# A planner that counts transfers in flight, and reciprocals of the third pair of heads spread by matrix products

## The chip, the cores and the metric

The kernel runs on one core of a Trainium2 chip. A core has five engines, each with its own row of instructions that it works off in order: TensorE (matrix products, PE in the profile, its weight loads PEld), VectorE (DVE), ScalarE (ACT), GpSimd (POOL) and SyncE (SP, which here only starts transfers). They wait for one another by semaphores. Data move between DRAM and the on-chip memory by DMA transfers that an engine issues; the queues are those of SyncE and GpSimd. TensorE writes to eight banks of its own (128 partitions x 512 floats each), from which VectorE and ScalarE read.

The metric is the device time of one execution in microseconds. Before the change three runs took 1011.58, 1011.61 and 1008.52 us, median 1011.58.

## The reference

Causal attention with a decay, for 8 batches x 8 heads, 576 positions, 64 numbers per head, then a two-layer network over all 4608 rows. All numbers are float32.

```python
scores = (1 / sqrt(64)) * q @ k.T                      # per batch and head
cum    = cumsum(log(clip(f, 1e-4, 1)))                 # f: one number per position
scores = where(later position, -1e9, scores + cum[:, None] - cum[None, :])
scores = scores - max(scores)
attn   = exp(scores);  attn = attn / (sum(attn) + 1e-9)
x      = (attn @ v)                                    # heads side by side: 4608 x 512
h      = x @ w_in                                      # 512 x 2048   (FFN1)
g      = max(h, 0) + alpha * min(h, 0)
out    = g @ w_out                                     # 2048 x 512   (FFN2)
```

## The kernel before

**Pairs of heads.** Attention is done for two heads at a time; 32 pairs, n = 0 to 31, four to a batch. For a pair TensorE makes the scores (q by k, five blocks of query rows, the last of 64 rows called the tail), VectorE adds the decay and takes the row's extreme (lines 609, 703 and 846), ScalarE takes the exponential and its row sums (571, 826). The first nine pairs (`attention`) turn the exponentials round by TensorE transposes (584, 651, 725), the other 23 (`turned`) by VectorE transposes (883) and 16 DMA moves (920), half of them issued by SyncE and half by GpSimd. Then come the value products with v, and ScalarE copies the result to `xs` (758, 959).

**Reciprocals.** The row sums of a pair lie down the partitions, and the values have the positions along the row. So the reciprocals (649) are transposed to nine rows of 128 (651), copied to `bR` (652) and spread over the partitions into `ri`, of which there is one buffer. For most pairs that is a store to DRAM (657) and three broadcast loads (1000, function `fetch`). The fourth pair (n = 3, `hurry`) does it by six products with a selecting matrix `sel` into two banks (function `quick`), and two VectorE copies (642) from there to `ri`. GpSimd multiplies `xs` by `ri` (979), ScalarE and GpSimd split the result into a high and a low part `xx` (988, 989): this is x of the pair, the input of FFN1.

**FFN1 and FFN2.** For a batch of 512 rows FFN1 has 16 chunks, each with two halves of six products of 512 columns: the first half takes x of the batch's first two pairs, the second half that of the last two. Nine such batches (the ninth gathers all 64-row tails) make 1728 products; their results go to DRAM (1039) and come back for FFN2, which runs when attention is over and has nothing but TensorE, VectorE and ScalarE work beside loads. While attention runs, FFN1's products fill TensorE between the products of the pairs.

**The order.** No order is written by hand. The kernel describes some 4170 operations, each with an engine, a cost in nanoseconds, a key, the operations it waits for and the buffers it takes; class `Plan` then plays the engines through: of all ready operations it takes the one that can start earliest, and of equal ones that with the lowest key. Every cost is first multiplied by a number drawn between 0.97 and 1.03 from one random sequence, operation by operation (`SEED`), so that one operation more or less shifts the draws of all that follow. A transfer ends when one common channel, at 220 or 280 bytes per nanosecond, has taken it. Rings of buffers (`Ring`) hold an operation back until one is free; the banks of transposes and spreading products are ring `rT`, of at most three. The order in which the planner takes the operations is the order of each engine's instructions; the waits in the program follow from the data alone. Up to 75 us, where the planner foresees TensorE idle for over 0.5 us, it also writes fillers (466), products of the identity matrix into a bank about to be used.

All products are written through the helper at line 364, so that their rows in the profile are told apart by tile names: `rqk` and `Qhl` are scores, `big,vr` values, `xx,wi` FFN1, `big,sel` spreading products.

Of the kernel before, what the change touches and what calls it, by code (L numbers as in the profile page):

```python
# [19 lines left out]
NP = H // 2  # L20
# [69 lines left out]

SLACK = {"DVE": 1.12, "ACT": 1.08, "POOL": 1.05}
ENGS = ("PE", "ACT", "DVE", "POOL", "SP", "-")


class Plan:
    def __init__(self):
        self.now = dict.fromkeys(ENGS, 0.0)
        self.chan = 0.0
        self.ops = []
        self.banks = self.fill = None  # L100
        self.rnd = random.Random(SEED)
# [27 lines left out]
    def run(self):  # L129
        ops, self.ops = self.ops, []  # L130
        cand = {e: [] for e in ENGS}
        for o in ops:
            if o.n == 0:
                cand[o.eng].append(o)
        left = len(ops)
        mine = set(ops)
        while left:
            best = None
            for e in ENGS:
                t0 = self.now[e]  # L140
                pick = None
                for o in cand[e]:
                    r = o.ready
                    for b in o.bufs:
                        if b.t is not None:
                            continue
                        k = b.seq - b.ring.next
                        if k and not any(o2.ring is b.ring and o2.seq == b.ring.next for o2 in o.bufs):
                            r = None
                            break  # L150
                        a = b.ring.at(k)
                        if a is None:
                            r = None
                            break
                        if a > r:
                            r = a
                    if r is None:
                        continue
                    s = t0 if t0 > r else r
                    if pick is None or (s, o.key) < pick[:2]:  # L160
                        pick = (s, o.key, o)
                if pick is not None and (best is None or pick[0] < best[0]):
                    best = pick
            assert best is not None, "the plan is stuck"
            s, _, o = best
            self.t = s
            cand[o.eng].remove(o)
            left -= 1
            end = s + o.ns
            t0_, new = self.now[o.eng], []  # L170
            if o.two:
                end += max(0.0, self.now["POOL"] - s)
            self.now[o.eng] = end
            if o.kb:
                self.chan = max(self.chan, s + 1.4) + o.kb / (220.0 if s < FAR else 280.0)
                end = self.chan + (0.0 if s < 4 else 2.0)
            o.start, o.end = s, end
            for b in o.bufs:
                if b.t is not None:
                    continue  # L180
                st = b.ring.store
                f = min(st.free)
                st.free.remove(f)
                b.i, b.t = f[1], st.items[f[1]]
                if o.eng == "PE" and st is self.banks:
                    new.append((f[0], b.t))
                b.ring.next += 1
                b.ring.held += 1
            if new and self.fill and s < FILL:
                self.fill(new[0][1], s - max(t0_, new[0][0]))  # L190
            o.fn()
            for b in o.bufs:
                b.left -= 1
                b.last = max(b.last, end)
                if b.left == 0:
                    b.ring.held -= 1
                    b.ring.store.free.append((b.last + 0.3, b.i))
            for c in o.outs:
                c.n -= 1
                c.ready = max(c.ready, end + self.lag(o, c))  # L200
                if c.n == 0 and c in mine:
                    cand[c.eng].append(c)
# [3 lines left out]
def attention_moe(  # L206
# [120 lines left out]
    def c_dve(n):  # L327
        return 75 + n / 0.96
# [216 lines left out]
    def attention(n):  # L545
# [2 lines left out]
        k0 = NS * n  # L548
        kl, kc = k0 - 16, k0 - 7
        hurry = HURRY if n == NP - 1 else 0  # L550


        held = []
# [70 lines left out]
        bri = Buf(rri)  # L624
        ri_ops = []

        def quick(bR, r_, key):

            bB = [Buf(rT), Buf(rT)]
            at = lambda c0: bB[c0 // 512].t[:, c0 % 512 : c0 % 512 + (128 if c0 < 512 else 64)]  # L630

            def prods():
                R9 = bR.t[0:9]
                for i in range(4):
                    mm(at(128 * i), sel[:, i], R9, True, True)
                mm(at(512), sel[:, 4], R9[:, 0:64], True, False)
                mm(at(512), sel[:, 5], R9[:, 64:128], False, True)

            q_ = op("PE", 1400, prods, key, [r_, o_sel], bB + [bR])
            quick_ops.append(q_)  # L640
            for c0, c1 in ((0, 512), (512, S)):
                ri_ops.append(op("DVE", c_dve(c1 - c0), lambda c0=c0, c1=c1: ve.tensor_copy(flat(bri)[:, c0:c1], bB[c0 // 512].t[:, 0 : c1 - c0]), key, [q_], [bB[c0 // 512], bri]))

        def quotients(key):

            bT, bR = Buf(rT), Buf(rR)
            both = lambda: su()
            q_ = op("ACT", 230, lambda: ac.activation(both(), both(), AF.Identity, bias=eps), key, sums + [o_eps], [bst])
            q_ = op("DVE", 190, lambda: ve.reciprocal(both(), both()), key, [q_], [bst])
            q_ = op("-", 400, lambda: None, key, [q_])  # L650
            t = op("PE", 109, lambda: pe.transpose(bT.t[0:9, 0:128], both(), ident), key, [q_, o_id], [bT, bst])
            r_ = op("ACT", c_act(128), lambda: ac.activation(bR.t, bT.t[0:9, 0:128], AF.Copy), key, [t], [bT, bR])
            if hurry:
                quick(bR, r_, key)
                return
            d = rd[n % 3][0 : 128 * 9]
            st_ = op("SP", 350, lambda: sy.dma_start(d.rearrange("(c q) -> c q", q=128), bR.t), key, [r_], [bR], kb=4.5)
            ri_ops.extend(fetch(key, st_, d, bri))
# [102 lines left out]
        v_deps = lambda: e1 + e2[0] + e2[1] + e3 + [e4, o_zero] + l_v  # L761

        def rest():
            st = k0 + 11.5 - hurry
            late = ri_ops if n < NN else [op("-", 2000, lambda: None, st, ri_ops)]
            quotient(n, bxs, bri, xs_ops[0] + xs_ops[1] + late, st)

# [24 lines left out]
            done(value_ops[-1])  # L792
        else:
            behind.append(values)
        quotients(k0 + 11 - hurry)
        later_x.append(rest)
        if n < NE - 1:
            for f_ in later_x:
# [7 lines left out]
    def turned(n):  # L806
# [110 lines left out]
        for i in range(16):  # L917
            a, k = i // 4, i % 4
            q_, n_ = (po, "POOL") if i % 2 else (sy, "SP")
            moves.append(op(n_, 550 if i % 2 else 450, lambda a=a, k=k, q_=q_: q_.dma_start(  # L920
                bM.t[32 * k : 32 * k + 32, a], t_t[32 * a : 32 * a + 32, k, 32 * TA * bTa.i : 32 * TA * bTa.i + CW]),
                k0 + 8.05, turns, [bTa, bTb, bM], kb=100))

# [476 lines left out]
```

## Time and profile before

| | before |
|---|---|
| three runs | 1011.58, 1011.61, 1008.52 us |
| profiled execution | 1010.48 us, its span 1008.7 us |
| TensorE busy | 999.0 us (99%) |
| weight loads busy | 888.5 us (88%) |
| VectorE, ScalarE, GpSimd busy | 803.7, 606.8, 394.6 us |
| TensorE in the chain that ended last | 93% |

The profiled execution is one of its own; the span runs from the first to the last instruction that the profile shows, and 1.8 us lie around it. A row in order of time gives the start, the time from its start to the end of the last of its instructions, the line, the tiles and the count; in square brackets stands the idle time before it and what ended it. Matmuls are pipelined and their ends modelled, so rows of TensorE overlap by a little. A float32 product that the program has once stands as two matmuls in the trace.

### The profile page before, as it was taken

Reading aid. Unit: us, or ns where it says so; the run is one execution under the profiler, and the core shown is the slowest. Engines: PE = TensorE matmul, PEld = TensorE weight load, DVE = VectorE, ACT = ScalarE, POOL = GpSimd, SP = SyncE. Lnnn points to the kernel's source line nnn. Section 1 sums busy time; section 2 is a strip of 40 time slices with the busy share of each in tenths; the row PEclk is TensorE's granted clock in tenths of the full one; section 3 lists DMA queues with packets and bytes.
Section 4 is the critical chain, followed back from the end, with each engine's and each line's share of the span. In section 5 each row is a group of like instructions: output and inputs, shape, how many; then the busy total and the mean of one; then the engine's idle time right before and its main releaser. Section 6 shows DMA issues by size and latency. Waiting matters only on the chain.

```text
span 1008.7 us, 22200 instructions
## 1 busy us (share of the span) xinstructions
PE 999.0 (99%) x7900; PEld 888.5 (88%) x7900; DVE 803.7 (80%) x1745; ACT 606.8 (60%) x1369; POOL 394.6 (39%) x635
## 2 busy tenths in 40 slices
PE   9999999999999999999999999999999999999998
PEld 6778888888888788888888888999999999999998
DVE  7878768888877848868655987788898888989994
ACT  7987876666666645656444766564554645546551
POOL 4575758799988858869740100000000000000000
PEclk9999999999999999999999999999999999999999
DMA  7988748889887887968766666633534344434411
GB/s 225 264 241 245 227 130 230 238 250 264 257 242 211 260 242 206 260 206 233 235 174 241 212 205 212 207 116 123 157 113 142 115 140 132 139 115 137 135 55 42
DMA packets 130686, 191.12 MB, mean 189 GB/s; under 512 B 22088, under 2 KB 79728, under 8 KB 130576
## 3 DMA queue, kind: packets, MB, share of 16 engines
q1 hardware_dynamic: 124400, 170.66, 55.7%
q0 software_dynamic: 5888, 18.85, 7.4%
q8 instruction: 62, 1.02, 0.4%
q14 instruction: 48, 0.39, 0.1%
q10 hardware_dynamic: 288, 0.20, 0.1%
HBM read 102.74 MB, written 48.80 MB: 150 GB/s over the span
## 4 chain that ended last, share of the span: by engine, by line
PE 93%; DMA 3%; DVE 2%; ACT 1%; SPq 1%; POOL 1%; issue 0%; DVEq 0%; ACTq 0%
PE bank L364 89%; PE bank L584 2%; DMA big<-big 1%; SPq L920 1%; DVE big L883 1%; DMA rd<-st 0%; DMA vr<-in_vv_dram 0%; PE bank L432 0%; DMA rqk<-in_qk_dram 0%; ACT big L826 0%; DVE Z L491 0%; PE bank L466 0%; POOL Z L510 0%; ACT big L580 0%; POOL Qhl L538 0%
## 5 line engine op out<-in xcount | busy, mean ns | idle before, releaser
L364 PE MATMUL bank<-xx,wi 128*128 128x512 f32 x1728 | 407.7, 392 | 1.8 <-DVE st L846 1.8
L364 PEld LDWEIGHTS bank<-xx,wi 128*128 128x128 f32 x1728 | 319.8, 188 | 68.4 <-DVE st L846 2.2
L826 ACT ACTIVATE big<-big,st 128x384 f32<-128x384 f32 (+4 forms) x207 | 118.6, 575 | 44.3 <-DVE st L846 44.3
L1037 DVE SCALAR_TENSOR_TENSOR hs<-bank,sa,hs 128x512 f32<-128x512 f32 x96 | 71.2, 743 | 79.0 <-ACT hs L1035 78.8
L364 PE MATMUL bank<-wi,gh 128*128 128x256 f32 x1008 | 123.9, 283 | 0.0
L364 PE MATMUL bank<-wot,gh 128*128 128x256 f32 x1008 | 123.9, 283 | 0.0
L364 PEld LDWEIGHTS bank<-wot,gh 128*128 128x128 f32 x1008 | 122.3, 192 | 0.1
L364 PEld LDWEIGHTS bank<-wi,gh 128*128 128x128 f32 x1008 | 122.3, 192 | 0.0
L1035 ACT ACTIVATE hs<-bank,ab 128x512 f32<-128x512 f32 x96 | 66.1, 689 | 88.3 <-PE bank L364 70.5
L883 DVE STREAM_TRANSPOSE big<-big 128x1408 f32<-128x1408 f32 (+2 forms) x69 | 86.6, 1273 | 22.3 <-DMA hd<-hs 6.7
L364 PEld LDWEIGHTS bank<-big,vr 128*64 128x64 f32 x1884 | 88.9, 137 | 12.0 <-issue 3.9
L364 PE MATMUL bank<-big,vr 128*64 128x128 f32 (+2 forms) x1884 | 95.5, 259 | 2.0 <-DVE st L609 1.1
L538 POOL TENSOR_TENSOR Qhl<-rqk,Qhl 128x640 fp32r<-128x640 f32 (+1 forms) x56 | 83.3, 1496 | 30.8 <-ACT Qhl L537 29.1
L920 POOL DMA_DIRECT2D big<-big x184 | 92.1, 507 | 7.9 <-DVE big L883 4.2
L364 PE MATMUL bank<-Qhl 64*128 64x512 f32 (+6 forms) x840 | 93.1, 326 | 0.1
L364 PEld LDWEIGHTS bank<-Qhl 64*128 64x128 f32 (+1 forms) x840 | 74.9, 186 | 15.8 <-issue 9.1
L510 POOL TENSOR_TENSOR Z<-Z,tri 128x384 f32<-128x384 f32 x60 | 54.6, 922 | 27.9 <-DMA Z<-c 18.5
L364 PE MATMUL bank<-wot,xx 128*128 128x256 f32 x504 | 62.4, 283 | 0.0
L364 PE MATMUL bank<-wi,xx 128*128 128x256 f32 x504 | 62.4, 283 | 0.0
L364 PEld LDWEIGHTS bank<-wi,xx 128*128 128x128 f32 x504 | 61.3, 192 | 0.0
L364 PEld LDWEIGHTS bank<-wot,xx 128*128 128x128 f32 x504 | 61.3, 192 | 0.0
L1032 ACT ACTIVATE hs<-bank,sg 128x512 f32<-128x512 f32 x48 | 33.0, 687 | 33.3 <-PE bank L364 28.4
(176 smaller groups left out, 1501.5 us busy)
## 6 DMA issues: line engine op xcount, KB each, us to landing
hd<-hs SPq DMA_DIRECT2D x144, 256.0 KB, 3.6
wx<-hd SPq DMA_DIRECT2D x46, 512.0 KB, 3.8
big<-big SPq DMA_DIRECT2D x184, 100.0 KB, 5.1
big<-big POOLq DMA_DIRECT2D x184, 100.0 KB, 4.9
rqk<-in_qk_dram SPq DMA_DIRECT2D x28, 608.0 KB, 5.1
hr<-hd SPq DMA_DIRECT2D x26, 512.0 KB, 3.5
vr<-in_vv_dram SPq DMA_DIRECT2D x32, 320.0 KB, 4.4
big<-in_w_in_dram SPq DMA_DIRECT2D x16, 512.0 KB, 6.1
```

The source lines that it names most:

```text
L364: pe.matmul(o, lhsT, rhs, start=start, stop=stop)
L510: m1 = op("POOL", c_po(128 * 3), lambda z4=z4: po.tensor_tensor(z4()[:, 6:9], z4()[:, 0:3], tb(3), ALU.add), kc + 0.1, got + [o_mask], [bZ])
L538: o2 = op("POOL", c_po(w), lambda hi=hi, lo=lo, raw=raw: po.tensor_tensor(lo(), raw(), hi().bitcast(F32), ALU.subtract), kc, [o1], [bqk, bQ])
L584: pe.transpose(t[:, c : c + 128], src[:, 128 * j : 128 * j + 128], ident)
L826: sums.append(op("ACT", c_exp(w), lambda: ac.activation(at(), at(), AF.Exp, bias=lo()[:, col : col + 1], scale=-1.0, accum_out=su()[:, col ...
L883: ve.transpose(t_t[:, :, c0 : c0 + 32 * (b1 - b0)].rearrange("p k (b c) -> p k b c", c=32), bE.t[:, 128 * off : 128 * (off + b1 - b0)].rea ...
L920: moves.append(op(n_, 550 if i % 2 else 450, lambda a=a, k=k, q_=q_: q_.dma_start(bM.t[32 * k : 32 * k + 32, a], t_t[32 * a : 32 * a + 32, ...
L1032: cp = op("ACT", c_act(512), lambda bh=bh, bs=bs, fc=fc: ac.activation(bs.t, bh.t, AF.Copy, scale=sg[:, fc : fc + 1]), -1000, [last, o_sg] ...
L1035: cp = op("ACT", c_act(512), lambda bh=bh, bs=bs, fc=fc: ac.activation(bs.t, bh.t, AF.Relu, scale=ab[:, fc : fc + 1]), -1000, [last, o_sg] ...
L1037: cp = op("DVE", c_dve(512), lambda bh=bh, bs=bs, fc=fc: ve.scalar_tensor_tensor(bs.t, bh.t, sa[:, fc : fc + 1], bs.t, ALU.mult, ALU.add), ...
```

## The change

Three edits. First, the planner keeps, for each queue, the list of the ends of its transfers (`flying`); where a queue has ten (SyncE, ScalarE) or eight (GpSimd) or more, a new transfer may not start before the tenth (eighth) last has ended. This is the planner's reckoning; no instruction is added for it. Second, SyncE's moves cost 550 in place of 450. Third, the third pair (n = 2) also goes the way of `quick`, its keys 15 lower; and `quick` takes one new bank instead of two, since its last 64 columns go into the bank of the transposed sums.

```diff
+DEEP = {"SP": 10, "POOL": 8, "ACT": 10}
 class Plan:
+        self.flying = {e: [] for e in DEEP}
...
                     s = t0 if t0 > r else r
+                    if o.kb and len(self.flying[e]) >= DEEP[e]:
+                        s = max(s, self.flying[e][-DEEP[e]])
...
                 end = self.chan + (0.0 if s < 4 else 2.0)
+                self.flying[o.eng].append(end)
...
         hurry = HURRY if n == NP - 1 else 0
+        soon = {NP - 1: HURRY, NP - 2: 15}.get(n, 0)
...
-        def quick(bR, r_, key):
-            bB = [Buf(rT), Buf(rT)]
-            at = lambda c0: bB[c0 // 512].t[:, c0 % 512 : c0 % 512 + (128 if c0 < 512 else 64)]
+        def quick(bT, bR, r_, key):
+            bB = [Buf(rT), bT]
+            at = lambda c0: bB[0].t[:, c0 : c0 + 128] if c0 < 512 else bT.t[:, 128:192]
...
-            if hurry:
-                quick(bR, r_, key)
+            if soon:
+                quick(bT, bR, r_, key)
                 return
...
-            st = k0 + 11.5 - hurry
+            st = k0 + 11.5 - soon
...
-        quotients(k0 + 11 - hurry)
+        quotients(k0 + 11 - soon)
...
-            moves.append(op(n_, 550 if i % 2 else 450, lambda a=a, k=k, q_=q_: q_.dma_start(
+            moves.append(op(n_, 550, lambda a=a, k=k, q_=q_: q_.dma_start(
```

The third pair's way costs one operation less than before, so the random draws of all later operations shift. Up to the transposes of the third pair the rows of all engines are the same; from there on they differ. Three places of TensorE's row follow. The changed kernel's line numbers are five or six higher (364 is 369 there, 466 is 471, 584 is 590, 651 is 657).

The first place is the third pair's transposed sums (line 651, written from `st_106`) and what follows them, before the change:

```order
L651 MATMUL bank_81<-big,st_106 9x128
L364 MATMUL bank_76<-rqk_94 128x288
L364 MATMUL bank_78<-rqk_94 128x288
L364 MATMUL bank_79<-big,vr_101 64x128 x14
L364 MATMUL bank_79<-big,vr_101 64x64 x10
L364 MATMUL bank_82<-big,vr_101 64x256 x2
L364 MATMUL bank_82<-big,vr_101 64x128 x2
L584 MATMUL bank_81<-big 128x128 x3
L584 MATMUL bank_76<-big 128x128 x3
L364 MATMUL bank_78<-rqk_94 128x512
L364 MATMUL bank_80<-rqk_94 128x512
```

and after it:

```order
L657 MATMUL bank_80<-big,st_106 9x128
L369 MATMUL bank_77<-rqk_94 128x384
L369 MATMUL bank_82<-rqk_94 128x384
L369 MATMUL bank_81<-rqk_94 128x288
L369 MATMUL bank_79<-big,sel 128x128 x4
L369 MATMUL bank_80<-big,sel 128x64 x2
L369 MATMUL bank_76<-big,vr_101 64x128 x14
L369 MATMUL bank_76<-big,vr_101 64x64 x10
L369 MATMUL bank_78<-big,vr_101 64x256 x2
L369 MATMUL bank_78<-big,vr_101 64x128 x2
L590 MATMUL bank_77<-big 128x128 x3
L369 MATMUL bank_82<-rqk_94 128x288
```

The spreading products (`big,sel`) are new behind the fourth pair's scores (`rqk_94`), and behind them the scores of the tail and the widest scores stand farther back, with three fillers between.

The second place is the fourth pair's transposed sums (from `st_104`) to its spreading products and the first products of FFN1, before:

```order
L651 MATMUL bank_81<-big,st_104 9x128
L466 MATMUL bank_77<-big 128x128 x5
...
L364 MATMUL bank_78<-big,vr_102 64x256 x2
L364 MATMUL bank_78<-big,vr_102 64x128 x2
L364 MATMUL bank_80<-xx,wi 128x512 x6
L364 MATMUL bank_79<-big,sel 128x128 x4
L364 MATMUL bank_83<-big,sel 128x64 x2
```

and after:

```order
L657 MATMUL bank_83<-big,st_104 9x128
L471 MATMUL bank_79<-big 128x128 x6
...
L369 MATMUL bank_81<-big,vr_102 64x256 x2
L369 MATMUL bank_81<-big,vr_102 64x128 x2
L369 MATMUL bank_78<-big,sel 128x128 x4
L369 MATMUL bank_83<-big,sel 128x64 x2
L369 MATMUL bank_76<-xx,wi 128x512 x6
```

The spreading products have moved ahead of FFN1's first six, and six fillers stand where five did.

The third place is the sixth of the pairs that are turned by moves, where the last scores of one pair (`Qhl_95`, 256 columns) meet the value products and the two tail scores of 320 and 256 columns, before:

```order
L364 MATMUL bank_81<-Qhl_95 128x256
L364 MATMUL bank_79<-Qhl_95 128x256
L364 MATMUL bank_83<-xx,wi 128x512 x6
L364 MATMUL bank_76<-big,vr_101 64x128 x20
L364 MATMUL bank_79<-big,vr_101 64x64 x10
L364 MATMUL bank_78<-Qhl_95 128x320 x3
L364 MATMUL bank_81<-Qhl_95 128x256 x3
L364 MATMUL bank_83<-xx,wi 128x512 x6
```

and after:

```order
L369 MATMUL bank_83<-Qhl_95 128x256
L369 MATMUL bank_76<-Qhl_95 128x256
L369 MATMUL bank_81<-big,vr_101 64x128 x20
L369 MATMUL bank_76<-big,vr_101 64x64 x10
L369 MATMUL bank_77<-Qhl_95 128x320 x3
L369 MATMUL bank_83<-Qhl_95 128x256 x3
L369 MATMUL bank_78<-xx,wi 128x512 x12
L369 MATMUL bank_82<-xx,wi 128x512 x12
```

Before, six FFN1 products stand between the scores and the value products; after, none does. Counted over all 23 such pairs, 11 had none there before and 15 have none after.

## Rows read from the trace of the kernel before

**Rows 1.** Page, busy time by engine and granted clock in 40 slices

```profile
PE 999.0 (99%) x7900; PEld 888.5 (88%) x7900; DVE 803.7 (80%) x1745; ACT 606.8 (60%) x1369; POOL 394.6 (39%) x635
...
PEclk9999999999999999999999999999999999999999
```

**Rows 2.** Page, shares of the chain that ended last, by engine

```profile
PE 93%; DMA 3%; DVE 2%; ACT 1%; SPq 1%; POOL 1%; issue 0%; DVEq 0%; ACTq 0%
```

**Rows 3.** By stretch: busy us of PE, PEld, DVE, ACT, POOL; clock, DMA share, GB/s

```profile
50.00:60.00 10.00, 8.93 (x101) 7.62 (x99) 8.35 (x23) 7.98 (x24) 6.78 (x6) 1.00 0.95 273
60.00:70.00 10.00, 9.25 (x71) 7.92 (x72) 6.79 (x21) 9.14 (x24) 9.18 (x11) 1.00 0.67 210
150.00:284.00 134.00, 133.78 (x1110) 111.86 (x1107) 112.08 (x276) 87.06 (x238) 116.73 (x191) 1.00 0.86 247
284.00:345.00 61.00, 58.39 (x507) 49.10 (x506) 45.33 (x107) 36.07 (x93) 50.83 (x82) 1.00 0.82 231
345.00:560.00 215.00, 215.00 (x1611) 181.88 (x1610) 146.17 (x335) 120.07 (x297) 136.48 (x219) 1.00 0.77 224
560.00:660.00 100.00, 100.00 (x513) 85.86 (x512) 80.79 (x144) 62.05 (x92) 0.00 (x0) 1.00 0.65 210
```

**Rows 4.** TensorE in order of time, 46 to 68 us: start, us, what

```profile
46.03 0.61 PE L466 MATMUL bank<-big 128*128 128x128 f32 x4
...
52.35 1.28 PE L466 MATMUL bank<-big 128*128 128x128 f32 x10
...
55.42 2.98 PE L364 MATMUL bank<-big,vr 128*64 128x128 f32 x56 [1.07 <-DVE st L609]
58.33 1.65 PE L364 MATMUL bank<-xx,wi 128*128 128x512 f32 x6
59.91 1.55 PE L364 MATMUL bank<-big,sel 9*128 9x128 f32 x12
...
66.42 0.66 PE L584 MATMUL bank<-big 128*128 128x128 f32 x4 [0.75 <-ACT big L580]
66.83 1.63 PE L364 MATMUL bank<-xx,wi 128*128 128x512 f32 x6
```

**Rows 5.** TensorE in order of time, later; last, the page's line on FFN1

```profile
302.70 4.27 PE L364 MATMUL bank<-xx,wi 128*128 128x512 f32 x18
...
313.89 8.45 PE L364 MATMUL bank<-xx,wi 128*128 128x512 f32 x36 [0.90 <-DVE st L846]
...
329.24 8.46 PE L364 MATMUL bank<-xx,wi 128*128 128x512 f32 x36 [0.86 <-DVE st L846]
...
340.57 2.98 PE L364 MATMUL bank<-big,vr 128*64 128x128 f32 x60 [0.76 <-DMA rd<-st]
...
535.87 106.38 PE L364 MATMUL bank<-xx,wi 128*128 128x512 f32 x468
...
L364 PE MATMUL bank<-xx,wi 128*128 128x512 f32 x1728 | 407.7, 392 | 1.8 <-DVE st L846 1.8
```

**Rows 6.** SyncE's queue in order of time; last, all moves of line 920

```profile
48.04 1.09 SPq L1000 DMA_DIRECT2D ri<-rd  x2
...
312.92 8.48 SPq L920 DMA_DIRECT2D big<-big  x8
...
L920 SPq DMA_DIRECT2D big<-big x184: 507/648/2370, 156.9 to 527.5; - x184
```

**Rows 7.** GpSimd in order of time; last, VectorE's copies of the fourth pair

```profile
46.58 1.44 POOL L979 TENSOR_TENSOR xs<-xs,ri 128x576 f32<-128x576 f32 x1
...
56.44 1.43 POOL L979 TENSOR_TENSOR xs<-xs,ri 128x576 f32<-128x576 f32 x1
...
60.13 1.27 POOL L989 TENSOR_TENSOR xx<-xs,xx 128x512 fp32r<-128x512 f32 x1 [0.50 <-ACT xx L988]
...
65.02 1.28 POOL L989 TENSOR_TENSOR xx<-xs,xx 128x512 fp32r<-128x512 f32 x1
...
61.16 0.82 DVE L642 COPY ri<-bank 128x512 f32<-128x512 f32 x2 [2.34 <-issue]
```

More of the change, by code (lines that the diff above doesn't have):

```diff
@@ L641, in quick @@
             for c0, c1 in ((0, 512), (512, S)):
-                ri_ops.append(op("DVE", c_dve(c1 - c0), lambda c0=c0, c1=c1: ve.tensor_copy(flat(bri)[:, c0:c1], bB[c0 // 512].t[:, 0 : c1 - c0]), key, [q_], [bB[c0 // 512], bri]))
+                ri_ops.append(op("DVE", c_dve(c1 - c0), lambda c0=c0, c1=c1: ve.tensor_copy(flat(bri)[:, c0:c1], bB[0].t if c0 == 0 else bT.t[:, 128:192]), key, [q_], [bB[c0 // 512], bri]))
         def quotients(key):
```

## The prediction

> **What bounds the kernel now.** I read the busy shares first [rows 1]: TensorE works 999.0 of 1008.7 us and its granted clock stands at the full level, 2.4 GHz, in all 40 slices, so no time is to be won from the clock. The chain that ended last agrees: 93% of it is TensorE [rows 2]. So the kernel's time is TensorE's work plus TensorE's idle time, and the question is where the 9.7 us of idle lie (1008.7 - 999.0). The table by stretches [rows 3] splits them: 1.07 and 0.75 us between 50 and 70 us, 0.22 us from 150 to 284 us (134.00 - 133.78), 2.61 us from 284 to 345 us (61.00 - 58.39), none from 345 to 660 us. What is left, 9.7 - 4.65 = 5.05 us, lies at the very start and at the end, which the change doesn't touch.
>
> A part of the busy time is no work. Where the planner foresees TensorE idle by over half a microsecond it writes products of the identity matrix, which nobody reads (line 466). Between 46.03 and 54 us there are 4 + 4 + 4 + 6 + 10 = 28 of them in the trace, the first and the last group shown [rows 4]; the last ten take 1.28 us, 0.128 us each, so the 28 take 3.6 us. What a new order can win is thus small: 3.6 us of fillers, 1.82 us of idle time between 50 and 70 us, and 2.83 us of waits later, 8.25 us in all.
>
> Is the busy rest really work? Far from any attention, 468 matmuls of FFN1 take 106.38 us [rows 5], 0.227 us each. The 36 that stand between two pairs of heads at 329.24 take 8.46 us [rows 5], 0.235 us each. Of the 1728 in all [rows 5] 1260 lie outside the long stretch, and at 0.008 us each they could hide some 10 us in the busy time; that is the upper end of what is hidden there.
>
> The Trainium skill ("Perfetto Trace Analysis", section "Identifying the Most-Contended Engine") goes further: the busy share of the matmuls does not tell how near TensorE is to its limit, that of the weight loads does. By that, 111.86 of 134 us from 150 to 284 us [rows 3] would leave 22 us to be won by a better order. This trace speaks against it here: from 560 to 660 us, with nothing but FFN1 and FFN2 and without any wait, the weight loads fill 85.86 of 100 us [rows 3], so most of the missing share is the shape of these matmuls and no room.
>
> **The change, part by part.**
>
> *The third pair's reciprocals (n = 2).* Gone are one store to DRAM and three broadcast loads, the first two at 48.04 us [rows 6], from SyncE's queue. Added are the six spreading products and two copies from a bank into the one buffer ri. The fourth pair does the same already: its products stand in the trace as 12 matmuls of 1.55 us together, at 59.91 us [rows 4]; its two copies take 0.82 us of VectorE [rows 7]. So TensorE gets 1.55 us more work. This is not hidden by itself: it stands in a row that is 99% busy, and can only take the place of idle time or fillers.
>
> What it brings is x of the third pair earlier. The loads were issued at 48.04 us, just when GpSimd's multiply for the second pair (46.58 + 1.44 = 48.02) had let go of ri [rows 6, 7]. The copies have to wait for that too, so they can't come before 48.0 and end near 48.9 us. GpSimd can then multiply near 49 to 51 us in place of 56.44 [rows 7], some 6 us earlier. Who waits for it? FFN1's first six matmuls (58.33 us [rows 4]) need the first two pairs alone. Its second half needs pairs three and four, and the fourth pair's x is ready only at 65.02 + 1.28 = 66.30 us [rows 7], the second half starting at 66.83 [rows 4]; the third pair's was ready at 60.13 + 1.27 = 61.40. Five microseconds of slack get six more. The gain is hidden behind the fourth pair.
>
> For the fourth pair the new order puts the spreading products ahead of FFN1's first six matmuls; before they stood behind them (58.33, then 59.91 [rows 4]). That is 59.91 - 58.33 = 1.58 us earlier on the path to its x, but the row ahead of it has become longer by the third pair's 1.55 us. These two cancel.
>
> *Fillers.* The planner now foresees more idle time around the third pair, as the products' two banks stay taken from the products until ri is free. The new row has 3 + 5 + 6 + 4 = 18 fillers in place of 2 + 2 + 2 + 3 + 5 = 14 (each row entry is two matmuls in the trace). Four more are 8 x 0.128 = +1.02 us.
>
> *The idle 1.82 us* waited for VectorE (1.07, a score bank not yet read, at 55.42) and for ScalarE (0.75, at 66.42) [rows 4]. In the new row fillers stand where these were. It can be 0 after (gain 1.82) or stay and grow to, say, double. I take half of it gone: -0.91.
>
> *The transfers in flight, and 550 in place of 450 for SyncE's moves.* Both are numbers for the planner: no wait is written into the program. The chip makes SyncE wait anyway: its eight moves from 312.92 take 8.48 us [rows 6], over 1 us each, while the shortest are half that (minimum 507 ns, median 648 ns [rows 6]). 450 was too little, 550 is nearer. What comes of it is another order from some 36 us on, in which the same work stands. The only price is in the waits that TensorE meets later, 2.83 us so far. Three of them (0.90, 0.86, 0.76 [rows 5]) stand at the pairs where scores, value products and tail scores follow one another without FFN1 between. The order before has 11 such places, two or three of them with a wait; the changed order has 15, among them again one series with only 18 FFN1 matmuls ahead of it, as at 302 us before. From below: all these waits vanish (-2.83). From above: the series costs its 2.52 us twice. Pro rata the waits are 15/11 x 2.52 = 3.44, +0.92; against that stands the truer cost of SyncE's moves, whose worth no row shows. I take 0 for this part and keep both ends.
>
> Of instructions changing tile shape there are about as many (168 before, 164 after), and the matmuls beyond those named are the same.
>
> **Sum.** +1.55 + 1.02 - 0.91 + 0 = +1.66 us on the profiled execution's 1010.48 us (span 1008.7 and 1.8 around it): 1012.1. That execution lies 1.10 us below the median of the three runs (1011.58; two of the three stand at 1011.6), so I add half of this: 1012.7 us. Against the median it is 0.1% slower; a difference below 0.3% (3.0 us) can't be told from no change.
>
> **Rivals.**
> - *The gain is real.* Idle time from 50 to 70 us and all later waits vanish: +1.55 + 1.02 - 1.82 - 2.83 = -2.08 on the profiled execution, 1008.4 us, or 1009.0 with the half. For it: fillers and idle time are where the change works, and the planner's queue is nearer to the chip. Against it: even then it is within 0.3%; more would need the fillers gone, and there are more of them. Chance 0.18, of which 0.07 over 0.3% faster.
> - *The series of pairs with little FFN1 between them stalls earlier and twice.* Changed order: from the sixth pair of this kind on, value products stand straight behind the scores, so in the stretch from 150 to 284 us, where the transfers are densest (DMA share 0.86 [rows 3]), and a second series stands at the end of attention. Each costs what the one from 302 to 341 us cost, 2.52 us, so two cost 2.52 more than now: 1012.7 + 2.5 = 1015.2, and 1016.1 if the idle 1.82 us stay as well. It decides from the point where the moves of a pair land after its scores have run, as at 340.57 us (0.76 us behind rd). Against it: from 345 to 560 us such places passed without any wait [rows 3]. Chance 0.28, nearly all of it slower.
> - *The change does not do what it says:* the limit of ten in flight seldom holds a transfer back, as the planner's own channel already spaces them; then only the products and a reshuffled order are left, and the sum is the forecast's.
> - *Room inside the busy time.* If the new order frees a third to all of the 10 us that FFN1's matmuls may hide between the pairs, the time is 1009 to 1003 us. For it: 0.235 against 0.227 us a piece. Against it: the matmuls' neighbours stay of the same kinds, and there are as many of them. Chance 0.03. (By the skill's rule above, a fifth of its 22 us would be 4 us.)
>
> **How the numbers follow.** Forecast 0.51, with the rival that changes nothing in it (its own range 1010.5 to 1014.5). Faster by over 0.3%: 0.07 + 0.03 = 0.10. Slower: 0.26 of the second rival and 0.04 of the forecast's upper end = 0.30. Within 0.3%: 0.60. The range goes from 1008.4, all waits gone, to two series stalling and some 1 us more, 1017.
>
> **What would show it.** Products of sel twice, 12 matmuls each, the first near 40 us and the second near 58 us; copies to ri near 48 us; 36 fillers after the first 10 us; GpSimd's third multiply before 52 us, and FFN1's second half still starting within 1 us of 66.8. TensorE's busy time up by 1.5 to 2.5 us. Of idle time from 150 to 560 us: 0 to 5 us, at pairs without FFN1 between scores and value products. It would be wrong if TensorE's idle time there passes 6 us, if FFN1's second half starts by 64 us or earlier, or if the same matmuls take another time per piece.

## The result, and the profile after

The changed kernel takes 1017.54 us (median of 13 runs, 1016.20 to 1019.74), the kernel before beside it 1012.14 us (median of 13, 1008.52 to 1017.89). The ratio is 1.0051, with a 95% interval of 1.0036 to 1.0066: half a per cent slower, where no change was forecast, and just above the range.

The profiled execution took 1016.32 us, its span is 1014.5 us, 5.8 us longer than before. The page of the changed kernel, busy time by engine and granted clock in 40 slices, against [rows 1]:

```profile
PE 1002.1 (99%) x7920; PEld 891.7 (88%) x7920; DVE 804.3 (79%) x1747; ACT 607.0 (60%) x1369; POOL 395.0 (39%) x635
...
PEclk9999999999999999999999999999999999999999
```

TensorE is busy 3.1 us longer (1002.1 against 999.0) and idle 2.7 us longer (12.4 against 9.7); its clock is at the full level in every slice. The same stretches as in [rows 3], of the changed kernel:

```profile
50.00:60.00 10.00, 8.04 (x83) 7.02 (x84) 9.38 (x30) 9.07 (x26) 8.06 (x8) 1.00 0.77 252
60.00:70.00 10.00, 10.00 (x101) 8.44 (x98) 6.43 (x19) 7.70 (x20) 7.60 (x10) 1.00 0.64 191
150.00:284.00 134.00, 130.34 (x1100) 109.80 (x1100) 105.97 (x257) 84.95 (x230) 113.35 (x181) 1.00 0.82 233
284.00:345.00 61.00, 61.00 (x500) 52.16 (x497) 47.06 (x118) 38.90 (x104) 49.20 (x82) 1.00 0.85 243
345.00:560.00 215.00, 213.43 (x1659) 179.20 (x1659) 145.78 (x339) 117.09 (x295) 140.53 (x229) 1.00 0.77 225
```

Between 50 and 70 us TensorE is idle for 1.96 us (1.82 before): one wait for VectorE in place of one for VectorE (1.07) and one for ScalarE (0.75). From 150 to 284 us 0.22 us of idle time have become 3.66; from 284 to 345 us 2.61 have become nothing; from 345 to 560 us nothing has become 1.57. TensorE in order of time, against [rows 4, 5], with the three long waits behind 200 us:

```profile
1.44 5.28 PE L437 MATMUL bank<-big 128*128 128x512 bf16 x12 [1.44 <-DVE big L434]
...
41.22 1.55 PE L369 MATMUL bank<-big,sel 9*128 9x128 f32 x12
...
54.72 1.50 PE L471 MATMUL bank<-big 128*128 128x128 f32 x12
...
58.90 2.98 PE L369 MATMUL bank<-big,vr 128*64 128x128 f32 x56 [1.96 <-DVE st L615]
61.81 1.55 PE L369 MATMUL bank<-big,sel 9*128 9x128 f32 x12
...
67.29 1.06 PE L471 MATMUL bank<-big 128*128 128x128 f32 x8
...
70.70 1.64 PE L369 MATMUL bank<-xx,wi 128*128 128x512 f32 x6
...
79.17 2.98 PE L369 MATMUL bank<-big,vr 128*64 128x128 f32 x56
...
214.91 2.19 PE L369 MATMUL bank<-Qhl 64*128 64x512 f32 x24
219.39 2.98 PE L369 MATMUL bank<-big,vr 128*64 128x128 f32 x60 [2.28 <-DMA rd<-st]
...
283.12 2.99 PE L369 MATMUL bank<-big,vr 128*64 128x128 f32 x60 [1.31 <-DMA vr<-in_vv_dram]
...
419.83 2.99 PE L369 MATMUL bank<-big,vr 128*64 128x128 f32 x60 [1.11 <-DMA rd<-st]
```

Two more waits of 0.26 and 0.18 us are not shown. Two rows of the kernel before, its first matmuls and the fifth pair's value products:

```profile
1.44 4.42 PE L432 MATMUL bank<-big 128*128 128x512 bf16 x12 [1.44 <-DVE big L429]
...
76.04 2.98 PE L364 MATMUL bank<-big,vr 128*64 128x128 f32 x56
```

The ledger of the 5.8 us: the program's first 12 matmuls 0.86 (5.28, 4.42 before; the program is the same there, and other kernels below, changed or not, have 4.06 to 5.30), the third pair's products 1.55, eight more fillers 1.0 (at 0.128 us each), the idle time at 50 to 70 us 0.14, the later waits 2.31 (5.14 in place of 2.83). Together 5.86; of busy time the rows give 3.4 us and the page 3.1, so single terms are good to some 0.3 us.

All three long waits stand at value products straight behind scores. Why the first is there shows in SyncE's queue. Of the changed kernel:

```profile
206.48 8.29 SPq L926 DMA_DIRECT2D big<-big  x8
214.87 0.53 SPq L937 DMA_DIRECT2D rd<-st  x1
...
269.71 9.10 SPq L926 DMA_DIRECT2D big<-big  x8
...
406.11 10.58 SPq L926 DMA_DIRECT2D big<-big  x8
```

and of the kernel before, first SyncE and then TensorE, for the same pair:

```profile
204.21 8.67 SPq L920 DMA_DIRECT2D big<-big  x8
```

```profile
213.94 2.19 PE L364 MATMUL bank<-Qhl 64*128 64x512 f32 x24
216.06 1.66 PE L364 MATMUL bank<-xx,wi 128*128 128x512 f32 x6
217.66 2.98 PE L364 MATMUL bank<-big,vr 128*64 128x128 f32 x60
```

Before, the last move's issue ended at 204.21 + 8.67 = 212.88, and the value products began 4.78 us later without a wait, behind six FFN1 matmuls. After, it ended at 206.48 + 8.29 = 214.77; the scores were done at 217.10, and the value products had to stand until 219.39, 4.62 us behind the issue. The profile puts the wait down to rd<-st, which is issued right behind the moves; the value products read what the moves bring. So the order before was on time with little to spare. The two rows at 269.71 and 406.11 belong to the other two long waits: there too the value products start a few microseconds behind the last issue (283.12 - 278.81 = 4.31 and 419.83 - 416.69 = 3.14). GpSimd's moves of the same three pairs had landed by 217.77, 281.65 and 418.01 us in the trace, 1.5 to 1.8 us before TensorE went on, so SyncE's were the late ones; not every landing of SyncE's is on record, and that its last move ends each wait is inferred from this. The page's rows on transfers (line, count, size, median us from issue to landing) say the same of all moves; first before, then after:

```profile
big<-big SPq DMA_DIRECT2D x184, 100.0 KB, 5.1
big<-big POOLq DMA_DIRECT2D x184, 100.0 KB, 4.9
```

```profile
big<-big SPq DMA_DIRECT2D x184, 100.0 KB, 5.7
big<-big POOLq DMA_DIRECT2D x184, 100.0 KB, 6.0
```

The planner reckons 1.4 us, the channel's time (100 KB at 280 bytes per ns, 0.36) and 2 us, 3.8 us together where the channel is free: 1.1 to 2.2 us less than these medians. For eight moves of SyncE it reckons 8 x 0.45 = 3.6 us of issuing before and 4.4 after; in these rows they take 8.3 to 10.6.

### The profile page after: what moved, and what is told of

The parts are those of the page before. It is cut to its first block, busy times and chain, and to the rows that moved or that the text cites. A ratio compares the mean times of both kernels' runs of the same rounds, so it can differ in the third digit from the quotient of the medians.

```text
span 1014.5 us, 22226 instructions
## 1 busy us (share of the span) xinstructions
PE 1002.1 (99%) x7920; PEld 891.7 (88%) x7920; DVE 804.3 (79%) x1747; ACT 607.0 (60%) x1369; POOL 395.0 (39%) x635
## 3 DMA queue, kind: packets, MB, share of 16 engines
q8 instruction: 62, 1.02, 0.4%
## 4 chain that ended last, share of the span: by engine, by line
PE 92%; DMA 5%; DVE 2%; POOL 1%; issue 0%; ACT 0%; DVEq 0%; SPq 0%; POOLq 0%
PE bank L369 88%; PE bank L590 3%; DMA big<-big 1%; DMA vr<-in_vv_dram 1%; DVE big L889 1%; DMA rqk<-in_qk_dram 1%; DMA rd<-st 1%; PE bank L437 1%; PE bank L471 0%; POOL big L926 0%; DMA hd<-hs 0%; POOL xx L995 0%; DVE hs L1043 0%; ACT hs L1041 0%; POOL xs L988 0%
## 5 line engine op out<-in xcount | busy, mean ns | idle before, releaser
L995 POOL TENSOR_TENSOR xx<-xs,xx 128x512 fp32r<-128x512 f32 x32 | 41.9, 1319 | 30.4 <-ACT xx L994 28.5
```

What stands on the lines that cost most here:

```text
L995: xl = op("POOL", c_po(512), lambda: po.tensor_tensor(bx.t[:, 1], bxs.t[:, 0:512], bx.t[:, 0].bitcast(F32), ALU.subtract), st, [xh], [bxs, ...
```

## The experiments

The first theory was that the planner's new numbers (the limit on transfers in flight, and 550) brought the later waits. Its rivals: the third pair's products alone cost the time; or any other order of the same work does, even one that comes only from other random factors. Each time stands beside the kernel before, run on the same chip (1011.4 to 1011.8 us).

### One part at a time

The third pair's products without the planner's new numbers (from the changed kernel):

```diff
-                    if o.kb and len(self.flying[e]) >= DEEP[e]:
-                        s = max(s, self.flying[e][-DEEP[e]])
...
-                self.flying[o.eng].append(end)
...
-            moves.append(op(n_, 550, lambda a=a, k=k, q_=q_: q_.dma_start(
+            moves.append(op(n_, 550 if i % 2 else 450, lambda a=a, k=k, q_=q_: q_.dma_start(
```

> The third pair's products alone, with the planner's transfers unlimited and SyncE's moves at 450 as before. Theory A (the time went to TensorE's waits at value products that stand straight behind the scores, brought by the planner's new numbers, plus 2.3 us at the start from the third pair's products, fillers and a wait that stayed): 9 such places, so only the start is dearer, 1014 to 1015 us, waits from 150 to 560 us under 3 us. Theory B (the shifted random draws made a poorer order, whatever the edit): 1016 to 1018 us. Theory C (the third pair's products and the banks that they hold are the whole loss): 1016 to 1018 us, with the loss before 80 us.

Measured: 1015.89 us, ratio 1.0046 (1.0030 to 1.0063).

The planner's new numbers without the third pair's products (the fourth pair's `quick` keeps its one new bank):

```diff
-        soon = {NP - 1: HURRY, NP - 2: 15}.get(n, 0)
+        soon = {NP - 1: HURRY}.get(n, 0)
```

> The planner's edits alone (ten in flight, 550 for SyncE's moves); the third pair by DRAM as before, the random draws the same as before. Theory A: the row of TensorE has 18 pairs whose value products stand straight behind the scores (11 before), so waits from 150 to 560 us of 4 to 7 us and 1014 to 1016 us. Theory B: the draws are those of before, 1012 us. Theory C: 1012 us.

Measured: 1016.47 us, ratio 1.0051 (1.0034 to 1.0068). Its profiled execution has nine waits between 80 and 560 us, 9.8 us together.

The kernel before with the random draws behind the third pair shifted by one, as the change shifts them, and nothing else:

```diff
+            d, drawn = rd[n % 3][0 : 128 * 9], plan.rnd.getstate()
...
             ri_ops.extend(fetch(key, st_, d, bri))
+            if n == NP - 2:
+                plan.rnd.setstate(drawn)
+                for _ in range(3):
+                    plan.rnd.random()
```

> The kernel before with the random draws shifted by one behind the third pair, as the change shifts them, and nothing else. Theory A: 10 places straight behind the scores, so 1011 to 1014 us, waits from 150 to 560 us of 1 to 4 us. Theory B: 1015 to 1018 us. Theory C: 1012 us.

Measured: 1015.06 us, ratio 1.0041 (1.0024 to 1.0058). TensorE of this kernel in order of time, the longest of its waits, and the stretch from 150 to 284 us:

```profile
203.17 2.98 PE L364 MATMUL bank<-big,vr 128*64 128x128 f32 x60 [2.62 <-DMA rd<-st]
```

```profile
150.00:284.00 134.00, 128.29 (x1074) 107.59 (x1075) 104.19 (x253) 81.48 (x217) 113.16 (x181) 1.00 0.81 232
```

5.71 us of idle time in that stretch (0.22 before), from nothing but other factors between 0.97 and 1.03. It has 10 places where value products stand straight behind scores, the order before 11 and the changed one 15: their number does not tell, since what counts is whether the moves have landed.

The whole change, with one extra draw behind the third pair, so that all later operations get the factors that they had before:

```diff
                 quick(bT, bR, r_, key)
+                if n == NP - 2:
+                    plan.rnd.random()
```

> The changed kernel with one more draw taken behind the third pair, so that all later operations draw the numbers that they drew before. Theory A2: it is still another order (18 places straight behind the scores), with 4 to 7 us of waits from 150 to 560 us: 1016 to 1018 us. Theory B (the shift of the draws is the cause in the whole change): 1013 to 1014 us, the start's 2.3 us alone being left.

Measured: 1015.00 us, ratio 1.0044 (1.0023 to 1.0064), with 7.5 us of waits. Having the old draws back does not save the old order.

These waits are mostly of one kind. Value products that, by the profile, waited for a transfer make 3.5 of the 3.8 us of waits from 80 to 560 us with the third pair's products alone, 8.4 of 9.8 with the planner's numbers alone, 5.7 of 7.1 with shifted draws and 5.2 of 7.5 with the old draws back.

What follows: each part alone costs nearly what the whole costs, 4 to 5 us, and so does no part at all, with only the draws shifted. The parts don't add up, so most of the price is that of leaving the order before (where the third pair's products are in, their own work is in it too). The first theory fell.

The same was tried with another seed for the kernel before:

```diff
-SEED = 66
+SEED = 67
```

> The kernel before with another seed of the random factors (67 instead of 66) and nothing else; 16 value products stand straight behind scores in place of 11, 27 fillers in place of 28 matmuls' worth. My theory (the order before has few waits by the luck of its draws, any other draws meet moves that have not landed): 1013 to 1017, with 5 to 9 us of waits between 80 and 1000 us at value products. Rival (the shift of the draws in the experiment before was itself an unlucky one): 1010 to 1012.5, with waits of 2 to 4 us.

Measured: 1015.18 us, ratio 1.0035 (1.0023 to 1.0048). TensorE of this kernel:

```profile
202.51 2.98 PE L364 MATMUL bank<-big,vr 128*64 128x128 f32 x60 [0.92 <-DMA rd<-st]
...
218.56 4.65 PE L364 MATMUL bank<-big,vr 128*64 128x128 f32 x60 [3.02 <-DMA rd<-st]
...
320.14 8.48 PE L364 MATMUL bank<-xx,wi 128*128 128x512 f32 x36 [1.43 <-DVE st L846]
...
347.07 2.98 PE L364 MATMUL bank<-big,vr 128*64 128x128 f32 x60 [2.10 <-DMA vr<-in_vv_dram]
```

7.47 us of waits from 80 to 560 us. Beside shifted draws and seed 67, seed 66 is a lucky one for the kernel before; how often a seed does as well, two redraws cannot tell.

### Moves reckoned to land later

The second theory: the planner takes the moves for landed too early, so that in whichever order it makes, value products stand where theirs are still on the way. The changed kernel with 4 us instead of 2 behind the channel, for the moves (all transfers of 100 KB):

```diff
-                end = self.chan + (0.0 if s < 4 else 2.0)
+                end = self.chan + (0.0 if s < 4 else 4.0 if o.kb == 100 else 2.0)
```

> The changed kernel with one number more for the planner: a move is reckoned to land 4 us after the channel has taken it, in place of 2. The row of TensorE then has 5 places with value products straight behind the scores in place of 15. Theory A: TensorE's waits from 150 to 560 us fall from 5.1 us to under 1.5 us, 1013 to 1014 us. Theory B: another order by chance, 1015 to 1019 us. Theory C: unchanged, 1017 us, as the start is the same.

Measured: 1011.51 us, ratio 1.0003 (0.9993 to 1.0013): against the changed kernel's 1.0051 the whole loss is gone. The two stretches of this kernel show how:

```profile
150.00:284.00 134.00, 134.00 (x1099) 111.85 (x1099) 106.28 (x256) 86.21 (x231) 111.37 (x177) 1.00 0.82 234
284.00:560.00 276.00, 276.00 (x2180) 232.25 (x2179) 195.90 (x458) 158.64 (x401) 195.37 (x316) 1.00 0.78 230
```

No idle time at all. The weight loads fill 111.85 of 134 us in the first stretch, 111.86 in the kernel before. (By the rule of the Trainium skill, "Perfetto Trace Analysis", section "Identifying the Most-Contended Engine", weighed in the prediction, there would still be some 22 us of room, an estimate from 134 - 111.85.) TensorE's busy time lies between 999.0 and 1004.2 us in every order tried here, so none of them found such room.

The same line in the kernel before, and in the kernel before with shifted draws:

> The kernel before with the moves reckoned to land 4 us after the channel in place of 2, nothing else. Theory A2 (the planner reckons the moves too early; any order has waits at the value products, that of before had few of them by luck): 3 places straight behind the scores, the 2.8 us of waits from 150 to 560 us go, 1008 to 1009.5 us. Theory B2 (the order of before is good by itself and any other is worse): 1012 to 1016 us.

> As before with the moves at 4 us, and the random draws shifted by one as well. Theory A2: the shift alone cost 4 us; with the later landing it costs nothing: waits from 150 to 560 us under 1 us, 1008 to 1009.5 us, the same as without the shift. Theory B2: 1012 to 1016 us.

Measured: 1010.91 us, ratio 0.9990 (0.9981 to 0.9999), and 1008.02 us, ratio 0.9959 (0.9945 to 0.9974). In the first the waits at the moves are gone and two others have come, 2.02 us; TensorE in order of time:

```profile
224.06 2.11 PE L364 MATMUL bank<-xx,wi 128*128 128x512 f32 x8 [1.29 <-POOL xx L989]
...
277.61 2.58 PE L364 MATMUL bank<-big,vr 128*64 128x128 f32 x46 [0.73 <-DVE hs L1037]
```

That was a miss: the first is FFN1 running ahead of its x, the second is for VectorE, neither is for a move. In the second no wait is left from 80 to 560 us, and with the same draws a loss of 0.41% has become a gain of 0.41%: it beats both kernels.

The planner's new numbers with this landing, without the third pair's products (the two diffs above together):

> The changed kernel with the third pair's reciprocals by way of DRAM again and every move reckoned to land 4 us after the channel instead of 2; 21 fillers in place of 36 or so, 2 value products straight behind scores. My theory (the planner reckons the moves to land too early; the third pair's products and the fillers are the only lasting cost): no wait of TensorE over 0.3 us between 80 and 1000 us, and a time 1.5 to 3.0 us under that of the changed kernel with the same landing (1011.5), so 1008.5 to 1010.0. Rival (the third pair's way costs nothing lasting, its products only take the place of idle time): 1011 to 1012. Rival (this order is as bad as any other reshuffle): 1014 or more.

Measured: 1010.62 us (1008.45 to 1011.26), ratio 0.9987 (0.9976 to 0.9998). Its profiled execution is the fastest of its runs and has no wait from 80 to 560 us; its TensorE is busy 999.9 us, that of the same kernel with the third pair's products 1003.1. The median is above what was expected; what its other runs lose could not be seen, since only one is profiled.

### SyncE's issuing at its measured time

The kernel before with the moves of SyncE at 1000, the landing as it was:

```diff
-            moves.append(op(n_, 550 if i % 2 else 450, lambda a=a, k=k, q_=q_: q_.dma_start(
+            moves.append(op(n_, 550 if i % 2 else 1000, lambda a=a, k=k, q_=q_: q_.dma_start(
```

> The kernel before with SyncE's moves reckoned at 1000 instead of 450, about what eight in a row take there in the dense stretch (8.3 to 8.5 us), the landing left at 2 us. If the too short cost of issuing is the error, the waits between 80 and 1000 us vanish and the time is 1007 to 1010. If it is the landing alone, the order is one more reshuffle with moves that come too late now and then: 1013 to 1016, with 4 to 8 us of waits. In between, if both are a part of the same lateness: 1010 to 1012.

Measured: 1007.90 us (1007.65 to 1008.69), ratio 0.9961 (0.9949 to 0.9974). Its two stretches:

```profile
150.00:284.00 134.00, 133.92 (x1082) 111.71 (x1084) 106.94 (x256) 83.46 (x223) 111.68 (x179) 1.00 0.80 238
284.00:560.00 276.00, 276.00 (x2155) 232.46 (x2151) 201.35 (x468) 161.60 (x405) 191.80 (x311) 1.00 0.78 232
```

The waits are gone by this number as well. And in the changed kernel, 1000 in place of 550:

> The changed kernel with SyncE's moves reckoned at 1000 in place of 550, the landing left at 2 us; 25 fillers, 7 value products straight behind scores. If the short issuing time is enough as a cause (550 went in the right direction and not far enough), the waits between 80 and 1000 us vanish here as they did with 1000 in the order before: 1009.5 to 1012, the third pair's products left over. If that other run was a lucky order, this one has 4 to 8 us of waits and takes 1013 to 1017.

Measured: 1012.15 us, ratio 1.0004 (0.9994 to 1.0015). From 150 to 284 us 1.44 us of idle time, from 284 to 560 us none:

```profile
150.00:284.00 134.00, 132.56 (x1097) 110.83 (x1096) 105.66 (x257) 85.79 (x230) 113.25 (x179) 1.00 0.81 234
284.00:560.00 276.00, 276.00 (x2175) 232.53 (x2174) 198.54 (x461) 161.74 (x404) 193.80 (x314) 1.00 0.78 231
```

A little of the waits came back, 1.12 us of it for VectorE; the loss by the order did not. What stays between the versions with the third pair's products and those without is 1.0003 against 0.9959 with the later landing (shifted draws) and 1.0004 against 0.9961 with 1000, some 4.3 us. But these kernels differ in the planner's new numbers and the one-bank `quick` as well. Only one pair of kernels differs by the third pair's way alone, the changed kernel and the planner's numbers, both with the later landing: 1.0003 against 0.9987, 1.6 us. Their profiled executions are 3.6 us apart (spans 1010.3 and 1006.7 us), of which 1.55 are there at the first value products, where the two programs are still the same; first the one with the third pair's products:

```profile
23.24 2.98 PE L369 MATMUL bank<-big,vr 128*64 128x128 f32 x56
```

```profile
21.69 2.98 PE L369 MATMUL bank<-big,vr 128*64 128x128 f32 x56
```

So some 2 us are left for the third pair by the profiles, 1.6 by the medians, and its price is known to no better than 1.6 to 4.4 us. Either number makes the planner hold the value products back by a few microseconds, and either cures both orders. That the moves are reckoned too early is shown by these two ways and by orders that share nothing but the lateness; how the lateness divides between issuing and landing is not, since either alone was enough. Nor was the same delay tried on other transfers, to see whether any slack ahead of the value products would have done.

### The fillers

The changed kernel without fillers behind 40 us:

```diff
-FILL = 75.0
+FILL = 40.0
```

> The changed kernel without the 18 fillers of 40 to 75 us (the planner writes them only up to 40 us); all other instructions stand in the same order. If the fillers cost what they last: 2.3 us less than the changed kernel's 1017.5 us at the most, 1 us of it against the kernel before. If they stand in time that TensorE would wait anyway: 1017.5 us, with the idle time from 40 to 80 us up from 2.0 to some 4 us. If they keep the clock up: the granted clock falls below full behind these waits and the time rises to 1018 to 1020 us.

Measured: 1017.67 us, ratio 1.0057 (1.0036 to 1.0077), the same as the changed kernel. TensorE of this kernel, with the long wait of the fourth pair's row, and the stretch from 40 to 80 us:

```profile
57.80 4.44 PE L369 MATMUL bank<-big,vr 128*64 128x128 f32 x56 [2.32 <-DVE st L615]
62.18 1.55 PE L369 MATMUL bank<-big,sel 9*128 9x128 f32 x12
...
78.63 2.98 PE L369 MATMUL bank<-big,vr 128*64 128x128 f32 x56
```

```profile
40.00:80.00 40.00, 36.78 (x324) 29.74 (x322) 32.24 (x87) 34.14 (x93) 29.86 (x36) 0.96 0.75 226
```

Without its 36 fillers (some 4.8 us) TensorE waits 3.22 us there instead of 1.96, and the value products behind the wait take 4.44 us instead of 2.98 at a granted clock of 0.96 in the stretch. Against the changed kernel the wait ends 1.10 us earlier (0.93 without the first matmuls, which were 0.17 faster), the value products cost 1.47 us more, and the row from there to the fifth pair's value products is 0.91 us shorter: 78.63 against 79.17. So some 3 of the fillers' 4.8 us stood in time that is lost anyway, and most of what the rest would have given went into slower value products. Whether those were slower for want of the fillers is not shown: the kernel with 1000 has 4.44 us there with all its fillers in. Apart from the fillers every engine has its instructions in the same order as in the changed kernel, yet the waits from 80 to 560 us are 4.2 us in place of 5.1; two executions of one order can differ by that much.

## Why the prediction was wrong

**What bounds the kernel** was right: the 5.8 us are TensorE's, 3.1 of them work and 2.7 idle. The sum put the profiled execution 1.66 us up; of the 4.2 us that it missed, 2.31 are the later waits, 1.05 the idle time at 50 to 70 us, and 0.86 the first matmuls.

**The third pair's products**, +1.55: right in place and size (41.22 us, 1.55). That its x comes early and brings nothing was right too. GpSimd's multiply, against 56.44 us in [rows 7]:

```profile
51.31 1.43 POOL L985 TENSOR_TENSOR xs<-xs,ri 128x576 f32<-128x576 f32 x1
```

It is 5 us earlier, yet FFN1's second half starts at 70.70 us (66.83 before), later, since the row ahead of it had grown by more than the products.

**The fillers**, +1.02: right in count (36) and near in time. As a cost of their own they were misread: taken out, nothing was won in all, since more than half of their time stood in a wait and slower value products took most of the rest. The fifth pair's value products start at 79.17 us, 76.04 before; 0.86 of the 3.13 are the first matmuls, and the products and fillers alone (2.57) cover the rest. That the chain of the third and fourth pair itself became longer is not shown.

**Half of the idle 1.82 us gone**, -0.91: wrong, 1.96 us stood there. The wait for ScalarE went, with eight fillers at 67.29 us near its place; the wait for VectorE grew from 1.07 to 1.96 us, although 12 fillers stood ahead of it. The planner's numbers without the third pair's products have 1.76 us there, so most of the growth is not the third pair's.

**Transfers in flight, 550 and the new order, 0**: this step failed, and it decides. It took the planner's new numbers for a neutral reshuffle, "The only price is in the waits that TensorE meets later, 2.83 us so far", and put the mean of reshuffles at the value of the order before. The runs show that the order before is no mean: five other orders with the old landing and issuing times near the old ones (one part, the other, shifted draws, old draws back, another seed) lie 0.35 to 0.51% above it, three of them without any of the third pair's work (0.41, 0.51, 0.35). A reshuffle should have been put at +4 us, with the order before as a lucky end. In the changed kernel's own profile the term that was put at 0 measured 2.31 us.

**The second rival**, 1015.2 to 1016.1 us, named the mechanism (moves that land after the scores have run, in the dense stretch from 150 to 284 us) and came within 1.4 us of the measured time at its upper end; it was given 0.28. Against it stood that such places passed without a wait from 345 to 560 us. That was the survivor's evidence: in a tuned order one sees the places that fit. The row that spoke for it had been read, eight moves in 8.48 us [rows 6] against 3.6 reckoned, and should have weighed more. That 550 is nearer was true and too little: 1000 cures what 550 does not.

**Outside every step**: the first 12 matmuls took 0.86 us longer in the profiled execution. The instructions are the same there, and kernels with the planner's edits have anything from 4.17 to 5.30 us for them, so it is put down to the execution.

**Its own signs**: the busy time (up 3.1 us, 1.5 to 2.5 named) and the start of FFN1's second half (70.70 us, 66.8 named) failed; the idle time from 150 to 560 us, 5.23, passed the 5 named without reaching the 6 that would have refuted it.

## What to carry to other kernels

Where a planner with random factors has set an order and one seed was kept, that order may be a lucky draw: an edit can lose the luck first, as all five other orders here did, and its own worth shows only beside several other draws. Compare what the planner reckons for a transfer with the trace (issuing one by one, and issue to landing) before changing anything else: one number set to the measured one (1000 for 450) gave 0.4%, in the kernel before, and took away most of what the edit had lost. Fillers ahead of a wait are a gauge of it, and taking them out gives back less than they last; here, nothing.

## What was not expected of the hardware

After some waits of 1.8 to 3.5 us the same 56 or 60 value products take 4.4 to 4.65 us instead of 2.98, and after others not. TensorE's rows of three kernels, the third pair's products alone, the planner's numbers alone, and the changed kernel with 1000:

```profile
222.29 4.63 PE L366 MATMUL bank<-big,vr 128*64 128x128 f32 x60 [3.51 <-DMA hd<-hs]
```

```profile
220.30 4.55 PE L369 MATMUL bank<-big,vr 128*64 128x128 f32 x60 [2.08 <-DMA big<-big]
```

```profile
57.91 4.44 PE L369 MATMUL bank<-big,vr 128*64 128x128 f32 x56 [1.96 <-DVE st L615]
```

and a stretch of the second, with its granted clock:

```profile
221.00:226.00 5.00, 5.00 (x60) 4.84 (x57) 5.00 (x17) 2.95 (x10) 3.27 (x7) 0.66 0.85 268
```

0.66 over 5 us is a mixture of the two levels, 1.2 and 2.4 GHz. But the waits of 2.28 us in the changed kernel and of 2.62 us with shifted draws left the products at 2.98 us, and the wait of 1.96 us at the fourth pair is followed by 2.98 us in the changed kernel and by 4.44 us in the one with 1000. What decides it is open. A wait can thus be followed by a loss of some 1.5 to 1.7 us on top of its length.
